# Loads that wait for the fourth tile ahead, the last x before a decode's end, and a ring of banks moved by one

## The chip, the cores and the metric

The kernel runs on one core of a Trainium2 chip. The metric is the device time of one execution in microseconds (us); three runs of the kernel before gave a median of 846.01 us (845.52 to 846.19).

## What is computed

```python
def reference(q, k, v, w_in, w_out, w_in2, w_out2):     # q, k, v: (4, 8, 576, 64)
    gamma = 1 - 2.0 ** (-5 - arange(8))                 # one per head
    D = where(i >= j, gamma[:, None, None] ** (i - j), 0)
    x = ((q @ k.T) / 8 * D) @ v                         # retention: attention with a decay, no softmax
    x = x.transpose(0, 2, 1, 3).reshape(2304, 512)
    x = relu(x @ w_in) ** 2 @ w_out                     # 512 -> 2048 -> 512
    h = x @ w_in2
    return (h * clip(h + 3, 0, 6) / 6) @ w_out2
```

The weights come as 64-bit floats and are turned into 32-bit ones on the chip.

## The kernel before

**Three parts.** First the retention, in ten units: two pairs of batches, and for each pair five stretches of the sequence (four of 128 positions, one of 64). Then the first MoE block, in four passes (`FIRST`) over 16 chunks of the hidden dimension. Then the second block, in three passes (`SECOND`) with seven products for eight. The order of every engine's instructions is the order in which the program writes them (a manual schedule); waits between engines are put in where a tile is written or read.

**A unit of the retention.** `load_qk` and `load_kv` bring a tile of keys and queries for the scores (128 x 1024 floats, 512 KB) and a tile of keys and values, one of each for both batches of the pair. `scale_keys` multiplies the keys of a kv tile in place by the decay, on POOL (line 283). `scores` makes the products of keys and queries (PE, line 322) and DVE multiplies them with the decay (line 326). `values` multiplies these with the values (line 338), adds the product of scaled keys and values to the running sums (line 346, which reads what POOL scaled), and from the second stretch on adds the earlier stretches' part (line 354). `to_x` lets DVE write the result to `xall` (line 372). The main loop runs `scores(u)` ahead of `values(u - 1)`; after it come `values` and `to_x` of unit 9, the last parts of the decode of the second tile of `w_in` (`parts1`, on DVE lines 183 and 189), and the first products of the MoE (`emit_h`, line 439).

**Loads.** All of them are issued by SP in the order of the list `order`: the qk and kv tiles, two tiles of `w_in` among them, and five weight tiles at the end. `load_on(done)` issues the loads whose place has been given back by unit `done`; the first call issues all that need nobody's place. The semaphores of DMAs go round eight, so each DMA waits until the one eight before it has landed. A tile of `w_in` takes four DMAs, the last kv tile of a pair two.

**Banks.** Scores and values take PSUM banks in turn (`next_bank`) from a ring of seven (0 to 6); bank 7 holds the running sums. After the retention the ring is banks 4 to 7. The first pass of the MoE writes its products to banks 6 and 7 and sums its results in banks 0 to 5 (the last two, `ytail`, for the 256 positions beyond 512). In the second pass the first two chunks take banks 6 and 7, and from the third on they take banks from the ring. The ring's counter runs on over both parts.

```python
ring["n"] = 7                        # before the first unit
...
p = values(UNITS - 1)                # after the loop over the units
parts1.pop(0)()
to_x(UNITS - 1, p)
load_on(UNITS)
...
ring.update({"from": 4, "n": 4})
```

Of the kernel before, what the change touches and what calls it, by code (L numbers as in the profile page):

```python
# [9 lines left out]
F32 = mybir.dt.float32  # L10
# [65 lines left out]
def retention_moe_moe2(ctx, tc, qk, qk_last, kv, w_in, w_out, w_in2, w_out2, consts, out):  # L76

    nc = tc.nc
# [10 lines left out]
    const = pool("const", 1)  # L89
# [29 lines left out]
    def bank(i, shape, name):  # L119
        return banks.tile(shape, F32, tag=f"b{i}", name=name)  # L120

    ring = {"at": 0, "from": 0, "n": 6}

    def next_bank(shape, name):
        ring["at"] += 1
        return bank(ring["from"] + ring["at"] % ring["n"], shape, name)


    staged = {}
# [74 lines left out]
    UNITS = (B // 2) * NTB  # L204
# [5 lines left out]
    def unit(u):  # L210

        p, i = divmod(u, NTB)
        return 2 * p, i, min(C, S - C * i)

    def make_decays():

        for e, engine in enumerate((nc.vector, nc.gpsimd)):
            engine.tensor_tensor(
                out=decay[:, e], in0=mask.unsqueeze(1).to_broadcast([128, HP, C]),
                in1=gv[:, e].unsqueeze(2).to_broadcast([128, HP, C]), op=ALU.mult,  # L220
            )
# [9 lines left out]
    def half(i):  # L231
        return slice(64 * i, 64 * i + 64)
# [3 lines left out]
    def space(u, k, which):  # L236

        b, i, n = unit(u)
        s = u // NTB * (2 * TILES + 1) + 2 * i + k
        if AHEAD <= s < AHEAD + WIDE:  # L240
            if not wide:
                wide.append(place("xr", [128, 2 * WIDE, 1024], F32, "early"))
            return wide[0][:, 2 * (s - AHEAD) + which]
        tags = TOKENS[s if s < AHEAD else (s - WIDE) % len(TOKENS)]
        name = ("qkt", "kvt")[which]
        if tags is None:
            return wop.tile([128, 1024], F32, tag="wo", name=name)
        return place(tags[which], [128, 1024], F32, name)

    def load_qk(u, k):  # L250
        b, i, n = unit(u)
        t = space(u, k, 0)
        if n == C:
            nc.sync.dma_start(out=t, in_=qk[b + k, i])
            data[u]["qk", k] = t.rearrange("p (e a t) -> p e a t", e=2, a=HP)
            return
        t = t.rearrange("p (b f) -> p b f", b=2)
        nc.sync.dma_start(out=t, in_=qk_last[b:b + 2].rearrange("b p e a t -> p b (e a t)"))
        for e in range(2):
            data[u]["qk", e] = t[:, e].rearrange("p (e a t) -> p e a t", e=2, a=HP)  # L260

    def load_kv(u, k):
        b, i, n = unit(u)
        t = space(u, k, 1)
        if n == C:
            t = t.rearrange("p (e h d) -> p e h d", e=2, h=H)
            nc.sync.dma_start(out=t, in_=kv[b + k, C * i:C * i + n])
            data[u]["k", k], data[u]["v", k] = t[:, 0], t[:, 1]
            return
        for e in range(2):  # L270
            nc.sync.dma_start(
                out=t[half(e), :H * D], in_=kv[b + e, C * i:, 1].rearrange("t h d -> t (h d)")
            )
        data[u]["v", 0] = t[:, :H * D].rearrange("p (h d) -> p h d", h=H)

    def scale_keys(u):
        b, i, n = unit(u)
        if n < C:
            return
        gk = cst[:, C_GK + H * i:][:, :H]  # L280
        for k in range(2):
            keyt = data[u]["k", k]
            nc.gpsimd.tensor_tensor(
                out=keyt, in0=keyt, in1=gk.unsqueeze(2).to_broadcast([128, H, D]), op=ALU.mult
            )
# [3 lines left out]
    def column(a, e):  # L289

        return a % 2 if a < 2 else 1 - (a % 2 ^ e)
# [36 lines left out]
    def values(u):  # L328
        b, i, n = unit(u)
        r = rets.pop(u)  # L330
        p = [next_bank([128, 2, 2 * n], "vps").rearrange("p c (k t) -> p c k t", k=2) for j in range(2)]
        if i == 0:
            sums_of[b] = bank(7, [128, 2, HP, D], "sps")
        for k in range(len(r)):
            for a in PAIRS:
                for e in range(2):
                    to = p[a // 2][half(e ^ a // 2), column(a, e)]
                    nc.tensor.matmul(
                        out=to[:, k] if n == C else to.rearrange("p k t -> p (k t)"),
                        lhsT=data[u]["v", k][:, 2 * a + e, :], rhs=r[k][e][:, a],  # L340
                        start=k == 0 and a % 2 == 0, stop=i == 0, skip_group_check=True,
                    )
            if n == C:
                for a in range(HP):
                    for e in range(2):
                        nc.tensor.matmul(
                            out=sums_of[b][half(e), k, a, :],
                            lhsT=data[u]["k", k][:, 2 * a + e, :], rhs=data[u]["v", k][:, 2 * a + e, :],
                            start=i == 0 and k == 0 and a == 0, stop=True, skip_group_check=True,
                        )  # L350
        for k in range(2) if i else ():
            for a in PAIRS:
                for e in range(2):
                    nc.tensor.matmul(
                        out=p[a // 2][half(e ^ a // 2), column(a, e), k],
                        lhsT=every[half(e), i % 2, k, a, :], rhs=data[u]["qk", k][half(e), 1, a],
                        start=False, stop=True, skip_group_check=True,
                    )
        if n == C:
            for a in range(HP):  # L360
                nc.scalar.activation(
                    out=every[:, (i + 1) % 2, :, a], in_=sums_of[b][:, :, a], func=ACTF.Copy,
                    scale=cst[:, C_GS + HP * i + a:][:, :1],
                )
        return p

    def to_x(u, p):
        b, i, n = unit(u)
        for j in range(2):
            own = slice(2 * j, 2 * j + 2)  # L370
            x = xall[:, own].rearrange("p k (b s) -> p b k s", b=B)[:, b:b + 2, :, C * i:C * i + n]
            nc.vector.tensor_tensor(  # L372
                out=x, in0=p[j].rearrange("p c k t -> p k c t"), in1=gq[:, own, :n].unsqueeze(1).to_broadcast([128, 2, 2, n]), op=ALU.mult
            )
# [268 lines left out]
    def pair(j, p, flip, between):  # L643
# [83 lines left out]
    coming = halves + [  # L727
        (0, 1, 2 * p + e, w) for p in range(NPAIR) for e, w in ((0, 0), (1, 0), (0, 1), (1, 1))
    ]
# [7 lines left out]
    with tc.manual_schedule():  # L737
# [6 lines left out]
        order = [("qk", 0), ("kv", 0), ("qk", 1)]  # L744
        for u in range(2, UNITS):
            order += [("qk", u), ("kv", u - 1)]
        order = [(kind, u, k) for kind, u in order + [("kv", UNITS - 1)] for k in range(2 if unit(u)[2] == C else 1)]
# [4 lines left out]
        def release(kind, u, k):  # L752

            s = u // NTB * (2 * TILES + 1) + 2 * unit(u)[1] + k
            if kind == "w" or s < AHEAD + WIDE + 2:
                return -1
            return FREED[s]
# [4 lines left out]
                   == (s - len(TOKENS) if s - len(TOKENS) >= AHEAD + WIDE else s - len(TOKENS) - WIDE))  # L762
            for s in range(AHEAD + WIDE + 2, (B // 2) * (2 * TILES + 1))
        }
        loads_w = [2]

        def load_on(done):

            while order:
                kind, u, k = order[0]  # L770
                if release(kind, u, k) > done or kind == "w" and len(order) <= 5 and done < UNITS - 3:
                    return
                order.pop(0)
                if kind == "w":
                    load()
                else:
                    (load_qk if kind == "qk" else load_kv)(u, k)

        load_qk(0, 0)
        load_qk(0, 1)  # L780
        del order[:2]
        nc.scalar.dma_start(out=cst[:, :C_GQ], in_=consts[:, :C_GQ])
        rows = place("t6", [128, C_END - C_GQ], F32, "rows")
        nc.scalar.dma_start(out=rows[:2], in_=consts[:2, C_GQ:])
        load_on(-1)

        warm = bank(6, [128, 256], "warm")
        for _ in range(WARM):
            nc.tensor.matmul(out=warm, lhsT=zeros[:, :128], rhs=zeros, start=True, stop=True)

        ring["n"] = 7
        make_decays()
        scale_keys(0)
        lows, parts0, parts1 = [], [], []
# [32 lines left out]
        for u in range(UNITS):  # L827
# [6 lines left out]
            if u != 1:  # L834
                v = max(u - 1, 0)
                p = values(v)
# [5 lines left out]
                make_last_decay()  # L842
            at(u, True)
        p = values(UNITS - 1)
        parts1.pop(0)()
        to_x(UNITS - 1, p)
        load_on(UNITS)
        next_load()
        split_in(0, 1, nc.gpsimd)
# [81 lines left out]
        for k in range(total):  # L931
            j, p = divmod(k, NPAIR)
# [80 lines left out]
```

## Time and profile before

| | |
|---|---|
| median of three runs | 846.01 us |
| the profiled execution, its own time | 846.26 us |
| its span, from the first to the last instruction | 844.5 us |
| busy in the span: PE, DVE, ACT, POOL | 98%, 62%, 54%, 17% |
| mean granted clock of TensorE | 0.999 |
| moved by DMA | 183.47 MB, mean 217 GB/s |

The span leaves out 1.8 us of the execution around it. PE is TensorE's matmuls, PEld its weight loads, DVE VectorE, ACT ScalarE, POOL GpSimd, SP the engine that issues the loads. In a timeline a row gives the start, the time to the end, the engine, the line, the operation, what it writes and reads, the number of instructions merged, and in brackets the engine's idle time before it with what ended it; "issue" is time in which the engine waited for nothing that the profile shows.

### The profile page before, as it was taken

To read this page: it belongs to the slowest core of one execution; us is meant where nothing else is said; L and a number is where in the kernel's file an instruction comes from. 1 tells how busy PE (TensorE), PEld (TensorE's weight loads), DVE (VectorE), ACT (ScalarE), POOL (GpSimd) and SP (SyncE) were. 2 spreads that over 40 slices of the span, in tenths; PEclk is the share of its full clock that TensorE was granted. 3 is DMA by queue.
4 is the path that set the end of the run, shared out by engine and by line. 5 is a ranking of instruction groups with operands and counts; after the bars stand their busy time and mean duration, and the time that the engine had idled before them with its cause. 6 is when DMAs were issued, how large, how long until landed. Compare 5 with 4: busy or idle time off the path is not lost.

```text
span 844.5 us, 13270 instructions
## 1 busy us (share of the span) xinstructions
PE 830.8 (98%) x4932; PEld 721.9 (85%) x4932; DVE 521.9 (62%) x875; ACT 454.4 (54%) x847; POOL 142.5 (17%) x122
## 2 busy tenths in 40 slices
PE   9889999999999999999999999999999999999997
PEld 7888888888888888888888889898898889889886
DVE  5778777775777777687665644545644546534433
ACT  1238767676677777777665433345433345433332
POOL 2352323231432233233320000000000000000000
PEclk9999999999999999999999999999999999999999
DMA  9991666565678777877686464562864552954622
GB/s 362 370 324 58 194 181 194 181 189 192 244 263 308 254 246 264 301 277 253 231 289 239 173 220 164 175 211 88 310 226 163 189 197 88 331 206 160 205 95 76
DMA packets 67413, 183.47 MB, mean 217 GB/s; under 512 B 6802, under 2 KB 23314, under 8 KB 67348
## 3 DMA queue, kind: packets, MB, share of 16 engines
q1 hardware_dynamic: 66768, 181.69, 62.3%
q10 hardware_dynamic: 580, 0.92, 0.3%
q8 instruction: 39, 0.64, 0.3%
q14 instruction: 26, 0.21, 0.1%
HBM read 146.41 MB, written 36.18 MB: 216 GB/s over the span
## 4 chain that ended last, share of the span: by engine, by line
PE 88%; DMA 8%; ACT 2%; DVE 1%; issue 0%; POOL 0%; SPq 0%; ACTq 0%; DVEq 0%
PE yps L623 23%; PE hps L439 22%; PE yps L482 21%; PE hps L657 20%; DMA qkt<-in_qk_dram 3%; PE ytail L482 3%; DMA stage<-in_w_in_dram 2%; DMA qkt<-in_qk_last_dram 1%; DMA cst<-in_consts_dram 1%; DMA wo<-kept 0%; ACT r L460 0%; ACT r L459 0%; DVE w L189 0%; ACT a L170 0%; ACT r L171 0%
## 5 line engine op out<-in xcount | busy, mean ns | idle before, releaser
L623 PE MATMUL yps<-wo,g 128*128 128x512 f32 x864 | 226.4, 394 | 0.2 <-DMA wo<-kept 0.2
L482 PE MATMUL yps<-g,wo 128*128 128x512 f32 x768 | 195.5, 392 | 0.4 <-POOL wo L196 0.4
L623 PEld LDWEIGHTS yps<-wo,g 128*128 128x128 f32 x864 | 159.5, 188 | 24.2 <-ACT v L668 0.4
L482 PEld LDWEIGHTS yps<-g,wo 128*128 128x128 f32 x768 | 140.0, 188 | 28.0 <-POOL wo L196 3.6
L439 PE MATMUL hps<-xring,win 128*128 128x512 f32 (+1 forms) x720 | 153.4, 361 | 1.8 <-DVE xall L372 1.5
L439 PEld LDWEIGHTS hps<-xring,win 128*128 128x128 f32 x720 | 123.1, 189 | 23.1 <-DVE xall L372 1.6
L657 PE MATMUL hps<-xlast,win 128*128 128x384 f32 x576 | 116.1, 336 | 0.0
L657 PEld LDWEIGHTS hps<-xlast,win 128*128 128x128 f32 x576 | 103.2, 188 | 8.8
L676 DVE TENSOR_TENSOR u<-hps,u 128x384 f32<-128x384 f32 x48 | 26.8, 558 | 107.3 <-PE hps L657 107.3
L465 DVE TENSOR_TENSOR g<-r,g 128x512 fp32r<-128x512 f32 x64 | 47.2, 737 | 70.0 <-ACT g L461 69.6
L657 PE MATMUL hps<-xop,win 128*128 128x384 f32 x432 | 87.2, 336 | 0.0
L459 ACT ACTIVATE r<-hps 128x512 f32<-128x512 f32 x80 | 43.9, 549 | 73.8 <-PE hps L439 73.8
L670 ACT ACTIVATE g<-c 128x384 fp32r<-128x384 f32 x72 | 37.8, 525 | 84.3 <-DVE c L669 84.3
L657 PEld LDWEIGHTS hps<-xop,win 128*128 128x128 f32 x432 | 77.5, 188 | 6.6
L668 ACT ACTIVATE v<-c,three 128x384 f32<-128x384 f32 x72 | 44.4, 617 | 32.7 <-DVE c L676 31.4
L439 PE MATMUL hps<-xown,win 128*128 128x512 f32 x240 | 59.8, 390 | 0.7 <-ACT xall L491 0.7
L195 ACT ACTIVATE win<-w 128x512 fp32r<-128x512 f32 x64 | 39.7, 620 | 26.7 <-DVE w L189 26.7
L174 DVE TENSOR_SCALAR a<-a 128x512 f32<-128x512 f32 x64 | 38.8, 606 | 24.0 <-ACT a L170 24.0
L439 PEld LDWEIGHTS hps<-xown,win 128*128 128x128 f32 x240 | 44.8, 188 | 10.1 <-ACT xall L491 0.9
L695 ACT ACTIVATE c<-hps 128x384 f32<-128x384 f32 x24 | 11.8, 492 | 76.7 <-PE hps L657 76.7
L460 ACT ACTIVATE r<-r 128x512 f32<-128x512 f32 x80 | 47.2, 590 | 2.5
L669 DVE SCALAR_TENSOR_TENSOR c<-v,c 128x384 f32<-128x384 f32 x72 | 40.0, 555 | 13.4 <-ACT v L668 13.4
(94 smaller groups left out, 980.9 us busy)
## 6 DMA issues: line engine op xcount, KB each, us to landing
wo<-kept SPq DMA_DIRECT2D x96, 512.0 KB, 5.0
win<-kept SPq DMA_DIRECT2D x72, 512.0 KB, 3.7
kept<-ready SPq DMA_DIRECT2D x40, 512.0 KB, 4.2
stage<-in_w_out_dram SPq DMA_DIRECT2D x32, 512.0 KB, 4.2
kept<-wo SPq DMA_DIRECT2D x16, 512.0 KB, 5.1
stage<-in_w_in_dram SPq DMA_DIRECT2D x16, 512.0 KB, 4.1
qkt<-in_qk_dram SPq DMA_DIRECT2D x13, 512.0 KB, 7.9
kvt<-in_kv_dram SPq DMA_DIRECT2D x13, 512.0 KB, 8.5
```

The costliest lines, as they stand in the source:

```text
L174: nc.vector.tensor_scalar(out=a, in0=a, scalar1=LEAST, scalar2=MOST, op0=ALU.max, op1=ALU.min)
L195: lambda: nc.scalar.activation(out=hi, in_=src, func=ACTF.Copy),
L439: nc.tensor.matmul(out=h, lhsT=w[:, wp, kk * 128:kk * 128 + 128], rhs=xs[pos, kk][xp][:, o:o + n], start=m == 0, stop=m == 3 * KD - 1,)
L459: nc.scalar.activation(out=r, in_=hs[k], func=ACTF.Relu)
L460: nc.scalar.activation(out=r, in_=r, func=ACTF.Square)
L465: nc.vector.tensor_tensor(out=lo, in0=src, in1=hi.bitcast(F32), op=ALU.subtract)
L482: nc.tensor.matmul(out=p, lhsT=w[:, wp, m * 128:m * 128 + 128], rhs=g[pos, c][k][:, gpart, :size], start=c == 0 and e == 0 and not (k and ...
L623: nc.tensor.matmul(out=p, lhsT=gt[m // 3][:, gpart, m % 3 * 128:][:, :128], rhs=w[:, wp], start=first and e == 0, stop=last and e == 2,)
L657: nc.tensor.matmul(out=to, lhsT=wl[k][:, half, wp, o], rhs=x[:, xp, f], start=first and m == 0, stop=last and m == 5, skip_group_check=True,)
L668: nc.scalar.activation(out=v, in_=c, func=ACTF.Relu, bias=three)
L669: nc.vector.scalar_tensor_tensor(out=c, in0=v, scalar=6.0, in1=c, op0=ALU.min, op1=ALU.mult)
L670: nc.scalar.activation(out=hi, in_=c, func=ACTF.Copy)
```

## The change

Three edits. **Markers:** from the seventh tile on, each load of the list is preceded by a copy of one element (4 bytes) from the tile loaded four before it into a small tile `seen`, on the same queue. The copy reads that tile, so SP waits until it has landed. There are 37 of them. **Order:** `to_x` of the last unit stands ahead of the last part of the decode. **Ring:** its counter starts at 1 instead of 0.

```diff
     def load_qk(u, k):
...
-            return
+            return t
...
-        loads_w = [2]
+        landing = []
+        seen = const.tile([1, 64], F32, name="seen")
+
+        def behind():
+
+            n = len(landing)
+            if n >= 6:
+                nc.sync.dma_start(out=seen[:, n:][:, :1], in_=landing[n - 4])
...
                 order.pop(0)
+                behind()
                 if kind == "w":
+                    name = coming[0][1:]
                     load()
+                    t = staged[name].bitcast(F32)
                 else:
-                    (load_qk if kind == "qk" else load_kv)(u, k)
+                    t = (load_qk if kind == "qk" else load_kv)(u, k)
+                landing.append(t[:1, :1])
...
-        load_qk(0, 0)
-        load_qk(0, 1)
-        del order[:2]
+        for k in range(2):
+            kind, u, k = order.pop(0)
+            landing.append(load_qk(u, k)[:1, :1])
...
-        ring["n"] = 7
+        ring.update({"at": 1, "n": 7})
...
         p = values(UNITS - 1)
+        to_x(UNITS - 1, p)
         parts1.pop(0)()
-        to_x(UNITS - 1, p)
         load_on(UNITS)
```

In the listings below the number behind a tile's name tells tiles of one name apart, and DMAHW0 to DMAHW7 are the eight DMA semaphores.

First SP, from the seventh load on (the first six are the same). Before:

```order
L254 DMA qkt_107<-in_qk_dram 128x1024 [waits DMAHW0_49]
L254 DMA early_109<-in_qk_dram 128x1024 [waits DMAHW1_49]
L267 DMA kvt_111<-in_kv_dram 128x1024 [waits DMAHW2_49]
L267 DMA kvt_113<-in_kv_dram 128x1024 [waits DMAHW3_49]
L254 DMA early_109<-in_qk_dram 128x1024 [waits DMAHW4_49]
```

Now:

```order
L776 DMA seen_92<-kvt_100 1x1 [waits DMAHW4_49,DMAHW0_49]
L254 DMA qkt_109<-in_qk_dram 128x1024 [waits DMAHW1_49]
L776 DMA seen_92<-kvt_102 1x1 [waits DMAHW5_49,DMAHW2_49]
L254 DMA early_112<-in_qk_dram 128x1024 [waits DMAHW3_49]
L776 DMA seen_92<-qkt_104 1x1 [waits DMAHW6_49]
L270 DMA kvt_115<-in_kv_dram 128x1024
L776 DMA seen_92<-qkt_106 1x1 [waits DMAHW7_49]
L270 DMA kvt_118<-in_kv_dram 128x1024
```

Between two loads stands a marker, which waits for the tile four loads back (kvt_100 is the third tile loaded, qkt_109 the seventh).

Second POOL, the scaling of the keys of units 0 and 1. Before:

```order
L283 TENSOR_TENSOR kvt_99<-kvt_99,cst_81 128x512 [waits DMAHW4_49]
L283 TENSOR_TENSOR kvt_101<-kvt_101,cst_81 128x512 [waits DMAHW5_49]
L283 TENSOR_TENSOR kvt_111<-kvt_111,cst_81 128x512 [waits DMAHW2_49]
L283 TENSOR_TENSOR kvt_113<-kvt_113,cst_81 128x512 [waits DMAHW3_49]
```

Now:

```order
L287 TENSOR_TENSOR kvt_100<-kvt_100,cst_81 128x512 [waits DMAHW4_49,DMAHW0_49]
L287 TENSOR_TENSOR kvt_102<-kvt_102,cst_81 128x512 [waits DMAHW5_49,DMAHW2_49]
L287 TENSOR_TENSOR kvt_115<-kvt_115,cst_81 128x512 [waits DMAHW5_49,DMAHW4_49]
L287 TENSOR_TENSOR kvt_118<-kvt_118,cst_81 128x512 [waits DMAHW7_49,DMAHW6_49]
```

The second semaphore is that of the marker that reads the same tile: the scaling writes the element that the marker reads, and the marker is written ahead of it in the program. So it is for the twelve full kv tiles of units 0 to 3, 5 and 7. For units 6 and 8 the scaling is written first, and the marker, and with it the load behind it, waits for POOL.

Third, where the retention ends, DVE. Before:

```order
L372 TENSOR_TENSOR xall_83<-vps_919,cst_81 128x2x2x128 [waits PE_49]
L183 SCALAR_TENSOR_TENSOR a_882<-stage_675,a_882 128x512 [waits DMAHW2_49,DMAHW1_49,DMAHW7_49,DMAHW0_49,DVE_49]
L189 ISA w32_530<-a_882,r_883 128x1024 [waits DVE_49,Activation_49]
L372 TENSOR_TENSOR xall_83<-vps_975,cst_81 128x2x2x64 [waits PE_49]
L372 TENSOR_TENSOR xall_83<-vps_976,cst_81 128x2x2x64 [waits PE_49]
L174 TENSOR_SCALAR a_1008<-a_1008 128x512 [waits Activation_49]
```

Now:

```order
L376 TENSOR_TENSOR xall_83<-vps_957,cst_81 128x2x2x128 [waits PE_49]
L183 SCALAR_TENSOR_TENSOR a_920<-stage_704,a_920 128x512 [waits DMAHW5_49,DMAHW4_49,DMAHW6_49,DMAHW3_49,DVE_49]
L376 TENSOR_TENSOR xall_83<-vps_1013,cst_81 128x2x2x64 [waits PE_49]
L376 TENSOR_TENSOR xall_83<-vps_1014,cst_81 128x2x2x64 [waits PE_49]
L189 ISA w32_554<-a_920,r_921 128x1024 [waits DVE_49,Activation_49]
L174 TENSOR_SCALAR a_1046<-a_1046 128x512 [waits Activation_49]
```

The decode's end (line 189) stands behind the two writes of the last x. On PE, the third chunk of the second pass (products `hps` from `xown`) began with a wait for ACT before; with the ring moved it takes another bank, and its first wait is one for DVE at its third matmul, as it had before too.

## Rows read from the trace of the kernel before

**Rows 1.** The page, busy time of each engine.

```profile
PE 830.8 (98%) x4932; PEld 721.9 (85%) x4932; DVE 521.9 (62%) x875; ACT 454.4 (54%) x847; POOL 142.5 (17%) x122
```

**Rows 2.** Stretches: length, busy time (instructions) of each engine, granted clock, DMA share, GB/s.

```profile
5.00:64.00 59.00, 52.55 (x1123) 47.97 (x1122) 41.42 (x72) 15.58 (x43) 25.78 (x24) 1.00 1.01 361
64.00:87.00 23.00, 21.96 (x122) 18.79 (x122) 18.94 (x31) 20.08 (x39) 6.92 (x5) 1.00 0.29 88
...
210.00:844.00 634.00, 630.04 (x2989) 547.33 (x2987) 371.97 (x632) 328.95 (x597) 75.02 (x64) 1.00 0.61 215
```

**Rows 3.** The page, DMA queues: packets, MB, share of 16 engines.

```profile
q8 instruction: 39, 0.64, 0.3%
```

**Rows 4.** Timeline of PE, the five stalls put down to "issue".

```profile
30.37 0.88 PE L338 MATMUL vps<-ret,early 128*64 128x128 f32 x12 [1.68 <-issue]
...
37.01 0.46 PE L354 MATMUL vps<-qkt,state 64*64 64x64 f32 x15 [0.83 <-issue]
...
43.71 0.51 PE L322 MATMUL aps<-qkt 64*128 64x128 f32 x3 [0.34 <-issue]
...
50.60 0.60 PE L322 MATMUL aps<-qkt 64*128 64x128 f32 x6 [0.77 <-issue]
...
56.77 0.45 PE L305 MATMUL aps<-qkt 64*64 64x64 f32 x14 [0.71 <-issue]
```

**Rows 5.** DMA queues in 27.8 to 29.2, 34.5 to 36, and 58.5 to 60 us.

```profile
q8 instruction: 1, 0.02, 4.8%
...
q8 instruction: 1, 0.02, 4.6%
...
q8 instruction: 1, 0.02, 3.9%
```

**Rows 6.** Timeline, units 0 and 1: POOL's scaling, PE's reading, SP's issues.

```profile
7.55 1.04 POOL L283 TENSOR_TENSOR kvt<-kvt,cst 128x512 f32<-128x512 f32 x1 [0.88 <-DMA kvt<-in_kv_dram]
...
9.86 0.63 PE L346 MATMUL sps<-kvt 128*64 128x64 f32 x16
...
11.34 0.33 SPq L267 DMA_DIRECT2D early<-in_kv_dram  x1
...
16.51 1.04 POOL L283 TENSOR_TENSOR kvt<-kvt,cst 128x512 f32<-128x512 f32 x1 [6.64 <-DMA kvt<-in_kv_dram]
...
16.58 1.09 PE L338 MATMUL vps<-ret,kvt 128*64 128x128 f32 x16 [0.97 <-DMA kvt<-in_kv_dram]
```

**Rows 7.** Timeline, units 7 and 8: POOL, and PE's reading of the last scaled keys.

```profile
50.13 1.81 POOL L196 TENSOR_TENSOR xring<-xall,xring 128x768 fp32r<-128x768 f32 x1
...
55.75 1.04 POOL L283 TENSOR_TENSOR kvt<-kvt,cst 128x512 f32<-128x512 f32 x1 [0.53 <-DMA kvt<-in_kv_dram]
...
59.53 0.63 PE L346 MATMUL sps<-kvt 128*64 128x64 f32 x16
```

**Rows 8.** Timeline, the end of the retention and the first product of the MoE.

```profile
62.16 0.69 PE L354 MATMUL vps<-qkt,state 64*64 64x64 f32 x32
62.44 0.68 DVE L183 SCALAR_TENSOR_TENSOR a<-stage,a 128x512 int32<-128x512 int32 x1
63.26 0.69 DVE L189 CUSTOM_DVE_ANT_0 w<-a,r 128x1024 uint16<-128x1024 uint16 x1
63.87 0.75 DVE L372 TENSOR_TENSOR xall<-vps,cst 128x256 f32<-128x256 f32 x2
63.99 0.63 ACT L195 ACTIVATE win<-w 128x512 fp32r<-128x512 f32 x1 [2.57 <-DVE w L189]
64.34 4.11 PE L439 MATMUL hps<-xring,win 128*128 128x512 f32 x21 [1.49 <-DVE xall L372]
...
67.41 0.60 ACT L459 ACTIVATE r<-hps 128x512 f32<-128x512 f32 x1 [0.54 <-PE hps L439]
```

**Rows 9.** Timeline, the third chunk of the second pass.

```profile
206.39 0.60 ACT L491 ACTIVATE xall<-ytail 128x512 f32<-128x512 f32 x1 [0.28 <-PE ytail L482]
...
207.04 0.50 PE L439 MATMUL hps<-xown,win 128*128 128x512 f32 x1 [0.69 <-ACT xall L491]
```

More of the change, by code (lines that the diff above doesn't have):

```diff
@@ L255, in load_qk @@
             data[u]["qk", k] = t.rearrange("p (e a t) -> p e a t", e=2, a=HP)
-            return
+            return t
+        whole = t
         t = t.rearrange("p (b f) -> p b f", b=2)
@@ L260, in load_qk @@
             data[u]["qk", e] = t[:, e].rearrange("p (e a t) -> p e a t", e=2, a=HP)
+        return whole
     def load_kv(u, k):
@@ L265, in load_kv @@
         if n == C:
+            whole = t
             t = t.rearrange("p (e h d) -> p e h d", e=2, h=H)
@@ L268, in load_kv @@
             data[u]["k", k], data[u]["v", k] = t[:, 0], t[:, 1]
-            return
+            return whole
         for e in range(2):
@@ L274, in load_kv @@
         data[u]["v", 0] = t[:, :H * D].rearrange("p (h d) -> p h d", h=H)
+        return t
     def scale_keys(u):
```

## The prediction

> **What bounds the kernel now.** I read the page's busy times first: TensorE is busy 830.8 of 844.5 us [rows 1], so only some 14 us of the span can be won without taking matmul work away. The stretches then say where they lie [rows 2]. From 210 us on PE is busy 630.04 of 634 us. In 5 to 64 us, the attention part, it is busy 52.55 of 59, and the DMA engines are full (share 1.01, 361 GB/s). In 64 to 87 us ACT is busy 20.08 of 23. The granted clock is 1.00 in all three, the higher of the two levels (2.4 GHz), so no term here is a clock term. Nothing of the change touches the work after 87 us except one bank.
>
> In the attention part the idle time of PE has two kinds. One is a wait for a load: 0.97 us at 16.58 [rows 6]. The other is put down to "issue", a wait for nothing that the profile shows: 1.68, 0.83, 0.34, 0.77 and 0.71 us, ending at 30.37, 37.01, 43.71, 50.60 and 56.77 [rows 4], 4.3 us in all. They come 6 to 7 us apart, in the middle of runs of matmuls whose operands are there. The queue table names the likely cause: 39 transfers of instructions, 0.64 MB [rows 3], 16 KB each; PE's 9,864 matmuls and weight loads [rows 1] make about 253 for each. One such transfer lies in 27.8 to 29.2 us and one in 34.5 to 36 us [rows 5], each ending 1 to 2 us before a stall ends [rows 4]. So PE runs out of instructions, and the next 16 KB don't begin to move until about 4.2 us after the last stall's end (30.37 to the window from 34.5). Where the loads thin out, the transfer lies in 58.5 to 60 us [rows 5], about 2 us after the stall that ended at 56.77, and no stall follows. The fetch shares the DMA engines with up to eight queued loads, and fewer queued loads should let it start sooner.
>
> **The change, part by part.**
>
> *The markers, what they give.* A load now follows a 4-byte copy that waits for the tile four loads back, so about four loads of 512 KB stand in the queues instead of eight. A load lands every 1.28 us (7.55 to 11.34 is three of them [rows 6]), so the four hold 5.1 us of work. A new load reaches the engines after two issues of about 0.33 us and its own start, while three loads, 3.8 us, still stand queued: the engines should stay fed, and I cost lost bandwidth at nothing; its cover is these 3.8 us. If the fetch then waits 2 instead of 4 us, all five stalls go: **-4.3 us**. Its bounds are -4.3 and 0.
>
> *The markers, what they cost.* There are 37, each a small issue on SP, which waits between loads anyway: nothing. But a marker reads the first element of a tile that POOL later scales in place. By the second listing of the change above, the scaling of the keys of units 0 to 3, 5 and 7 now waits for the marker as well as for the load. The marker is issued when the tile has landed and stands behind the three loads issued since, so it lands some 3.8 us later. Unit 0: POOL scaled at 7.55, when the tile landed; the third load behind that tile is the one whose landing released SP at 11.34. So the scaling runs from about 11.4 to 12.45, and the product that reads it, at 9.86 before [rows 6], starts **2.6 us** late. That makes the 0.97 us wait of unit 1 vanish (-1.0): its tile has long landed. Unit 1's scaling, 16.51 before, may come up to 3.8 us later and end at 21.35; PE, 1.6 us late, would want it at 19.2. If the copy stands on a DMA engine that is ahead, the wait is less; between 0 and 2.1 I take **1.0**. Units 2 and 3 then lie behind a PE that is 2.6 us late, and wait for nothing. By unit 5 the lost stalls have brought PE back, and units 5 and 7 may wait 0 to 1.5 us each; I take **0.5** twice. After unit 7 POOL still has its 1.81 us split [rows 7] ahead of the next keys. Sum of the attention part: -4.3 + 2.6 - 1.0 + 1.0 + 1.0 = **-0.7 us**. Its last product, 62.16 + 0.69 = 62.85 before [rows 8], ends near 62.15.
>
> The Trainium skill (DMA: Bandwidth & Descriptors, "Queues, rings and completion order") says that each DMA engine consumes its descriptors in ring order: by that the marker stands behind the loads, as I have it. No row of before shows a copy of this size.
>
> *The last x and the bank.* The first matmul of the MoE waited 1.49 us for DVE's write of the last x, since it reused that bank [rows 8]. With the ring moved by one its bank was read units ago, and it starts when PE is free. But ACT sets the pace there. Its weight copy at 63.99 waits for the decode that ended at 63.26 + 0.69 = 63.95, and then four decode copies run to 66.87. The decode step now stands behind the last x (0.75 us), which can start only at 62.4, when DVE's step before it is done: 62.4 + 0.75 + 0.69 gives about 63.9, no earlier than before. So ACT is free at 66.87 as before, and only the 0.54 us that it then waited for PE [rows 8] go. **The 0.7 us shrink to 0.55**; PE's 1.49 us turn into waits for ACT, whose bank read gates the next groups.
>
> *The bank in the second block.* At 207.04 PE had waited 0.69 us for ACT's copy out of a tail bank (at 206.39) [rows 9]. With the ring one further this group takes a bank last read two groups earlier, and the first matmul's wait for ACT is gone from PE's order: **-0.7 us**, and PE is the bound from there [rows 2].
>
> Sum: -0.55 - 0.7 = -1.25 us. The profiled execution took 846.26 us (844.5 and 1.8 around it), 0.25 above the median of 846.01. From the median: **844.7 us**.
>
> **The rivals.** A: *the marker lands at once*, because its engine is ahead or it overtakes. Then the key waits are 0 and the loads bound the part: unit 8's second keys, scaled from 55.75 to 56.79, were read at 59.53 [rows 7], so 2.7 us can be won there. With the 0.15 us lost at ACT and 0.7 us of the bank: **842.7**. For it: the DMA engines needn't be equally late; against: all are full.
>
> B, the slower side: *the fetch starts no sooner*. If an engine alternates between the fetch's queue and the loads' queue, its wait depends on what one turn holds and not on how many loads stand behind. Then the 4.3 us of stalls stay and the key waits come on top: 844.7 + 4.3 = **849.0**. It decides if the fetch still starts about 4 us after a stall's end. For it: with eight loads, 10 us of work, the fetch waited about 4.2, so it does overtake some; against: where fewer and smaller loads were queued it waited about 2 [rows 4, 5]. The Trainium skill (same page and section) has this as its rule: an engine round-robins between queues and switches only at packet boundaries, of some 9 to 17 descriptors. By that rule queue depth would not matter and the time would be B's; that the wait exceeded a load's 1.28 us neither fits one short packet nor excludes longer ones.
>
> C: *the markers change nothing that ends last*; gains and waits cancel and only the bank of the second block counts: 846.0 - 0.7 = **845.3**.
>
> The Trainium skill (Runtime: NRT & Kernel Launch, "Instruction fetch mechanics") calls fetches of 16 KiB blocks mostly hidden; the trace agrees on the size and, with five stalls in this part, disagrees on the hiding.
>
> **How the numbers follow.** Forecast 0.42, with 843.7 to 846.3 as its own range (each of the two unsure key terms at its ends); A 0.20; B 0.26; C 0.12. A measurement of this kernel tells about 0.2% (1.7 us) from no change, so faster means below 844.3. That is A and somewhat under half of the forecast's range: 0.38. Slower is B: 0.26. The rest, 0.36, is within. The range reaches just past A to 842.0 and up to B's 849.0.
>
> **What would show it.** Right: no "issue" idle time above 0.3 us on PE between 5 and 64 us; POOL's first scaling starts near 11.4 instead of 7.55; the last product of the attention ends near 62; the first MoE matmul follows it without a gap; PE's 0.69 us gap near 206 is gone. POOL's first scaling near 9 would speak for A; stalls of 0.7 us and more, a block of instructions apart, and a last product after 65, for B. Wrong altogether: a DMA share well under 0.95 in the attention part, which would mean that four loads don't keep the engines fed.

## The result and the profile after

The changed kernel took 854.06 us in the median of five runs (853.05 to 854.76), the kernel before, run beside it, 845.52 (845.15 to 846.19). The ratio is 1.0092, with a 95% interval of 1.0080 to 1.0103: slower by 8.5 us, where I had forecast a gain of 1.3 and no case above 849. The profiled execution of the changed kernel has a span of 852.1 us, 7.6 more than before. Two executions far off the rest, 2129.73 us of run 4 below and 1024.75 of the kernel before, are left out of every figure.

The page, busy time of each engine; PE has 1.6 us more work than in [rows 1], which is the same work at a lower clock in places:

```profile
PE 832.4 (98%) x4932; PEld 723.0 (85%) x4932; DVE 523.2 (61%) x875; ACT 454.4 (53%) x847; POOL 143.4 (17%) x122
```

The stretches of the changed kernel (length, busy time and instructions of PE, PEld, DVE, ACT and POOL, granted clock, DMA share, GB/s):

```profile
5.00:64.00 59.00, 47.41 (x926) 42.70 (x930) 35.48 (x59) 11.02 (x31) 19.70 (x18) 0.94 0.93 317
...
9.00:12.20 3.20, 0.43 (x8) 0.19 (x4) 0.00 (x0) 0.04 (x1) 1.04 (x1) 0.85 1.02 396
12.20:16.00 3.80, 3.77 (x50) 3.65 (x50) 1.25 (x2) 0.04 (x1) 1.04 (x1) 0.50 0.93 370
20.00:35.00 15.00, 13.47 (x318) 12.38 (x314) 10.17 (x19) 2.28 (x8) 5.55 (x6) 1.00 0.92 303
...
64.00:87.00 23.00, 20.48 (x281) 17.89 (x272) 19.78 (x32) 17.73 (x37) 10.96 (x10) 1.00 0.46 136
210.00:844.00 634.00, 633.85 (x3012) 551.12 (x3011) 374.47 (x636) 332.68 (x604) 75.28 (x64) 1.00 0.61 214
```

Against [rows 2] the loss lies in the attention part. In 5 to 64 us PE is busy 47.41 us instead of 52.55 and gets through 926 matmuls instead of 1123. The DMA engines, full before, moved 317 GB/s instead of 361, their share fell from 1.01 to 0.93, and the granted clock from 1.00 to 0.94. What PE waited for there, in the view of waits (what waited, for what: us in total, times, longest):

```profile
PE sps L350 <- POOL kvt L287: 9.4, 4, 3.3
PE sps L350 <- POOL early L287: 1.9, 1, 1.9
PE vps L342 <- POOL ret L304: 0.2, 1, 0.2
```

No "issue" row is left: the five stalls of [rows 4] are gone. All that PE waits for is keys that POOL has still to scale, 11.3 us, and POOL waited for the markers. (The view names a load for one of POOL's waits, the one before the scaling at 45.39; but SP issued that tile's marker at 40.62, after the tile had landed, so there too it is the marker that came late.) Its timeline (start, us, engine, line, operation, idle time before with what ended it):

```profile
11.13 1.04 POOL L287 TENSOR_TENSOR kvt<-kvt,cst 128x512 f32<-128x512 f32 x1 [4.48 <-DMA seen<-kvt]
...
19.55 1.04 POOL L287 TENSOR_TENSOR kvt<-kvt,cst 128x512 f32<-128x512 f32 x1 [6.11 <-DMA seen<-kvt]
```

These answer to 7.55 and 16.51 of [rows 6]. What followed on PE in unit 0, from its timeline:

```profile
8.34 1.09 PE L342 MATMUL vps<-ret,kvt 128*64 128x128 f32 x16
12.23 1.12 PE L350 MATMUL sps<-kvt 128*64 128x64 f32 x16 [2.80 <-POOL kvt L287]
13.14 1.92 PE L342 MATMUL vps<-ret,kvt 128*64 128x128 f32 x16
14.85 1.07 PE L350 MATMUL sps<-kvt 128*64 128x64 f32 x16
15.85 3.98 PE L326 MATMUL aps<-qkt 64*128 64x128 f32 x48
```

The wait itself is 2.80 us, but behind it the same matmuls take longer: 1.12 us where the product of [rows 6] took 0.63, and so on for four groups. The stretch 12.2 to 16 above has a clock of 0.50, the lower level of 1.2 GHz, after a stretch in which PE was busy for 0.43 of 3.20 us. Over the four groups this adds 2.8 us (for each, its time less that of the same group before: 0.49, 0.88, 0.44 and 1.03).

The end of the retention, which answers to [rows 8]:

```profile
70.31 0.69 PE L358 MATMUL vps<-qkt,state 64*64 64x64 f32 x32
70.94 4.44 PE L443 MATMUL hps<-xring,win 128*128 128x512 f32 x24
71.66 0.74 DVE L376 TENSOR_TENSOR xall<-vps,cst 128x256 f32<-128x256 f32 x2
72.33 0.67 DVE L189 CUSTOM_DVE_ANT_0 w<-a,r 128x1024 uint16<-128x1024 uint16 x1
```

The last product starts at 70.31, 8.15 us later than before. The terms: stalls -4.33, unit 1's wait for its load -0.97, first matmuls 0.6 shorter, key waits +11.4, POOL's `ret` +0.2, lower clock +2.8; together +8.5, which leaves 0.4 to rounding and overlap. The first MoE matmul then follows without the gap of 1.49 us.

### The profile page after: what moved, and what is told of

Read it like the earlier page. It is cut to its first block, busy times and chain, and to the rows that moved or that the text cites. A ratio compares the mean times of both kernels' runs of the same rounds, so it can differ in the third digit from the quotient of the medians.

```text
span 852.1 us, 13333 instructions
## 1 busy us (share of the span) xinstructions
PE 832.4 (98%) x4932; PEld 723.0 (85%) x4932; DVE 523.2 (61%) x875; ACT 454.4 (53%) x847; POOL 143.4 (17%) x122
## 4 chain that ended last, share of the span: by engine, by line
PE 88%; DMA 6%; ACT 1%; POOL 1%; DVE 1%; SPq 1%; issue 1%; ACTq 0%; DVEq 0%; POOLq 0%
PE yps L627 24%; PE hps L443 21%; PE hps L661 21%; PE yps L486 20%; DMA kvt<-in_kv_dram 3%; PE ytail L486 2%; DMA qkt<-in_qk_dram 2%; POOL kvt L287 1%; SPq L776 1%; DMA early<-in_kv_dram 1%; DMA seen<-kvt 1%; DMA stage<-in_w_out_dram 0%; ACT r L171 0%; DVE a L183 0%; ACT r L464 0%
## 5 line engine op out<-in xcount | busy, mean ns | idle before, releaser
L195 ACT ACTIVATE win<-w 128x512 fp32r<-128x512 f32 x64 | 39.7, 620 | 28.0 <-DVE w L189 27.8
```

The lines of the kernel that those rows point to most:

```text
L195: lambda: nc.scalar.activation(out=hi, in_=src, func=ACTF.Copy),
```

## Experiments

In the records theory W is that the read of the key holds back the scaling and so makes the loss; its rival D, that four queued loads don't keep the DMA engines fed. Later records call the sharper form of D theory Q.

**1. Markers that read a value.** The tile is the same, the element one that POOL does not write, so the scaling no longer waits for the marker.

```diff
-                landing.append(t[:1, :1])
+                landing.append(t[:1, 512:513] if kind == "kv" and unit(u)[2] == C else t[:1, :1])
```

> The markers of the full kv tiles read the first value instead of the first key, which POOL does not write; all else as in the change. Theory W (the copy that reads a key holds back POOL's scaling until it has landed): no wait of POOL for a marker in units 0 to 3, PE's waits for scaled keys fall from 11.3 us to under 3, no fall of the clock at 9 to 18 us, last product of the retention near 60 us instead of 71, time 841 to 844 us. Rival D (four loads ahead starve the queues, so the loads themselves come late): DMA share still near 0.93, last product after 66 us, time 849 us or more.

Measured: 852.4 us, ratio 1.0063 (1.0041 to 1.0084). The key waits are all but gone and the clock is 1.00 throughout, but most of the loss stays. The stretch of 5 to 64 us, then the three longest of PE's waits in the timeline:

```profile
5.00:64.00 59.00, 50.35 (x1011) 43.75 (x1010) 38.29 (x67) 14.38 (x38) 20.75 (x19) 1.00 0.90 317
```

```profile
15.10 1.16 PE L326 MATMUL aps<-early 64*128 64x128 f32 x16 [1.04 <-DMA early<-in_qk_dram]
23.77 1.09 PE L342 MATMUL vps<-ret,kvt 128*64 128x128 f32 x16 [1.32 <-DMA kvt<-in_kv_dram]
...
36.37 1.25 PE L326 MATMUL aps<-qkt 64*128 64x128 f32 x16 [1.85 <-DMA qkt<-in_qk_dram]
```

PE now waits for the loads themselves, at the same 317 GB/s. Theory W falls for the greater part. The read of the key may add to it, 854.06 us with it and 852.4 without, but the two intervals of the ratio overlap between 1.0080 and 1.0084, so the times alone don't show it.

**2. Order and ring alone.** The kernel before, with the last x moved and the ring started at 1, and no markers.

```diff
-        ring["n"] = 7
+        ring.update({"at": 1, "n": 7})
...
+        to_x(UNITS - 1, p)
         parts1.pop(0)()
-        to_x(UNITS - 1, p)
```

> The kernel before with the order of the last x and the ring moved by one, without markers. Theory W: the retention is as before, PE's 0.7 us gap at 206 us is gone, the swap at the end of the retention is worth between -0.5 and +0.5 us: 844.6 to 845.8 us. Rival O (these two edits carry the loss): 849 us or more.

Measured: 845.34 us, ratio 0.9992 (0.9982 to 1.0001): not told from no change, and no part of the loss.

**3. Markers alone**, with order and ring as before (the reverse of the diff above, on the changed kernel).

> The change with the order of the last x and the ring undone: markers alone. Theory W: the same waits for scaled keys as in the change, and the 0.7 us gap near 206 us back: 854 to 855.5 us. Rival O: under 850 us.

Measured: 854.69 us, ratio 1.0091 (1.0068 to 1.0114). The markers carry the whole loss.

**4. Only unit 0 freed.** The markers of unit 0's kv tiles read a value, all others as in the change.

```diff
-                landing.append(t[:1, :1])
+                landing.append(t[:1, 512:513] if kind == "kv" and u == 0 else t[:1, :1])
```

> The change, but the two markers of unit 0's kv tiles read a value instead of a key: of the waits for scaled keys only that of unit 0 (2.8 us) is taken away. If the fall of the clock in 12 to 18 us comes from PE's idle time in that wait, it goes too (2.8 us more), and the sum of 5.6 us is partly taken back by later waits: 849 to 852 us, granted clock 1.00 in 5 to 20 us. If the clock falls for another reason, it falls again and the time is 852 us or more.

Measured: 854.71 us, ratio 1.0096 (1.0075 to 1.0117): a miss, nothing was won. Unit 0 no longer waits and the clock stays at 1.00 from 5 to 20 us, but a longer wait stands in unit 1, again with a fall of the clock behind it (0.77 in 20 to 35 us). PE's timeline:

```profile
22.54 1.12 PE L350 MATMUL sps<-kvt 128*64 128x64 f32 x16 [4.01 <-POOL kvt L287]
```

One wait taken away alone was followed by another at a later tile, as one would expect where the loads set the pace.

**5. Markers that read a constant.** All 37 stay, but none waits for a tile.

```diff
-                nc.sync.dma_start(out=seen[:, n:][:, :1], in_=landing[n - 4])
+                nc.sync.dma_start(out=seen[:, n:][:, :1], in_=cst[:1, :1])
```

> All 37 markers stay, but each copies one constant that landed before the first load, so no marker waits for a tile. Theory Q (the loss is the short queue, and the markers shorten it by being transfers themselves: SP keeps at most eight unfinished transfers, and every second one is now a marker): the load still waits for the fourth load ahead of it; 849 to 855, 310 to 330 GB/s in 5 to 64 us, key waits gone, PE waiting for loads, at most 1 us of issue stalls. Rival R (the loss is what the markers read, the wait for the tile four loads back): without it eight loads stand queued again, 844 to 847, 350 GB/s and more, and the issue stalls of some 4 us are back. Rival S (the 37 issues of 0.585 us on SP are the loss): loads are then issued no faster than every 0.9 us, which is less than the 1.28 us of one load, so at most 1 us, 845 to 847.

Measured: 850.01 us, ratio 1.0049 (1.0037 to 1.0061). The stretch, PE's longest wait in the timeline, and the longest total among SP's waits:

```profile
5.00:64.00 59.00, 52.27 (x1031) 47.37 (x1032) 40.51 (x67) 14.40 (x38) 23.63 (x21) 0.94 0.94 326
```

```profile
34.58 1.25 PE L326 MATMUL aps<-qkt 64*128 64x128 f32 x16 [2.53 <-DMA qkt<-in_qk_dram]
```

```profile
SPq L270 <- DMA kvt<-in_kv_dram: 5.3, 8, 2.0
```

As theory Q had it: 326 GB/s, PE waits for loads, no stall. A marker is itself one of the eight DMAs that SP may have unfinished, so the 37 of them shorten the queue to four loads whatever they read; SP's loads wait here for earlier loads, though no marker reads a tile. Rival R falls (it had 844 to 847), and so does S (845 to 847), the theory that the loss is the issues. About 1 us of the loss goes with falls of the clock (0.66 in 35 to 40 us, 0.58 in 60 to 64): the executions with a mean clock of 1.000 and 0.999 took 849.06 and 849.66 us.

Two parts of the stretch differ; two lines from this run, two from the change and two from the kernel before:

```profile
10.00:20.00 10.00, 8.78 (x176) 8.15 (x176) 6.83 (x12) 1.48 (x6) 2.15 (x3) 1.00 1.03 399
25.00:35.00 10.00, 7.47 (x199) 6.79 (x196) 5.37 (x10) 3.40 (x10) 3.06 (x4) 1.00 0.90 277
...
10.00:20.00 10.00, 7.77 (x104) 7.65 (x106) 3.33 (x6) 1.14 (x4) 2.53 (x3) 0.66 0.96 361
25.00:35.00 10.00, 8.47 (x204) 7.74 (x202) 6.17 (x12) 1.14 (x4) 3.72 (x4) 1.00 0.88 273
...
10.00:20.00 10.00, 9.03 (x194) 8.56 (x194) 6.84 (x12) 1.46 (x6) 2.08 (x2) 1.00 1.03 408
25.00:35.00 10.00, 8.32 (x216) 7.58 (x212) 5.11 (x10) 3.42 (x10) 3.06 (x4) 1.00 1.05 335
```

In 10 to 20 us, where this run and the change load each tile in one DMA of 512 KB, four places for loads keep the engines full if nothing waits for a tile to land (399 GB/s, and 408 before); with the wait for the landing, as in the change, it is 361. In 25 to 35 us both fall short alike, 277 and 273 against 335. Just before, SP has issued a tile of `w_in` as four DMAs (256, 128, 64 and 64 KB), and it issues a kv tile as two of 128 KB. The ring counts DMAs, so its places then hold fewer bytes: an estimate from the trace of this run, bytes issued less bytes moved, gives about 1.2 MB queued in 10 to 20 us and 0.6 in 25 to 35. This reason fits both parts, but no run varies it alone.

**6 and 7. A marker before every second load**, reading a value, that waits for the fourth or for the sixth load back. Of eight unfinished DMAs some five are loads.

```diff
-            if n >= 6:
-                nc.sync.dma_start(out=seen[:, n:][:, :1], in_=landing[n - 4])
+            if n >= 6 and n % 2 == 0:
+                nc.sync.dma_start(out=seen[:, n:][:, :1], in_=landing[n - 6])
```

> A marker only before every second load, waiting for the fourth load back (a value, not a key), so four to five loads stand queued. Theory Q: between the change with values (852.4) and before: 847 to 851, 325 to 350 GB/s in 5 to 64 us, few issue stalls. Rival R: half of the waits are gone, 847 to 850. Rival S: 845 to 847. A run at 852 and more would say that one load more in the queue is worth nothing.

> A marker before every second load, waiting for the sixth load back; of eight unfinished transfers some five are loads. Theory Q: 845 to 849, 335 to 355 GB/s in 5 to 64 us; if the fetch of instructions gains from three loads fewer, issue stalls of 1 to 3 us in place of 4. Rival R: 844 to 846. If four loads were already as good as five, it would be 851 to 853.

Measured: 849.89 us, ratio 1.0049 (1.0033 to 1.0066), for the fourth load back; 845.32, ratio 0.9997 (0.9988 to 1.0005), for the sixth. The stretch of 5 to 64 us, first of the one, then of the other:

```profile
5.00:64.00 59.00, 52.30 (x1083) 46.35 (x1084) 41.93 (x69) 15.52 (x42) 23.86 (x24) 1.00 0.95 340
```

```profile
5.00:64.00 59.00, 54.94 (x1132) 49.35 (x1132) 44.03 (x73) 15.73 (x43) 25.45 (x24) 1.00 0.98 351
```

Both lie where theory Q put them; by the times rival R had them there too, and it is run 5 that speaks against R. The pair has the same markers on the same queue and differs in what they wait for: two loads less of waiting are worth 4.6 us. So with half of the markers the read counts as well. The issue on SP is no price of weight at this number, since the same 19 issues stand in both and the second loses nothing.

**8. A marker before every third load, sixth load back** (`n % 3 == 0` in the diff above, all else as there). Six of the eight are loads.

> A marker before every third load, waiting for the sixth load back; of eight unfinished transfers six are loads. Theory Q: 843.5 to 847, 345 to 360 GB/s in 5 to 64 us; issue stalls of 2 to 4 us remain, since most of the queue is back. This is the point at which a gain over the kernel before (845.5) could show, if fed engines and an early fetch go together at all; if they do not, it stands at 845 to 846 with the stalls of before.

Measured: 844.02 us, ratio 0.9978 (0.9969 to 0.9987): faster than both kernels. The stretch, and PE's stalls and the end of the retention in its timeline:

```profile
5.00:64.00 59.00, 55.16 (x1135) 49.72 (x1135) 43.81 (x73) 16.25 (x44) 25.27 (x24) 1.00 0.99 359
```

```profile
29.09 0.88 PE L342 MATMUL vps<-ret,early 128*64 128x128 f32 x12 [0.44 <-issue]
...
48.88 1.38 PE L326 MATMUL aps<-qkt 64*128 64x128 f32 x19 [1.10 <-issue]
...
60.62 0.69 PE L358 MATMUL vps<-qkt,state 64*64 64x64 f32 x32
61.25 4.47 PE L443 MATMUL hps<-xring,win 128*128 128x512 f32 x24
```

Fed engines, and two stalls of 1.54 us instead of five of 4.33 [rows 4]: the retention ends 1.54 us sooner than in [rows 8]. It ends hardly sooner than in run 2, though, which has no markers (60.62 against 60.69), and the intervals of the two ratios overlap between 0.9982 and 0.9987. That the thinned markers win anything beyond the moved order and ring is therefore not shown.

**9. The thinned markers alone**, without the moved x and ring.

> The thinned markers (before every third load, sixth load back, a value) without the moved x and the moved ring. Theory Q with the instruction stalls: the markers alone win by the shorter queue, 844 to 845.3 (the run with all parts, 844.0, plus the 0.7 us that order and ring gave by themselves), issue stalls of 1 to 2 us, 350 to 360 GB/s. Rival: the gain of the thinned markers hangs on the moved x and ring, since the work after the attention sets the pace: then 845.3 to 846.5, no different from before.

Measured: 845.17 us, ratio 0.9992 (0.9983 to 1.0001). By the time alone neither case is excluded. In the profiled execution the last product starts at 60.93, 1.2 us sooner than before, and then the gain is lost. PE's timeline and the stretch behind it:

```profile
63.52 10.22 PE L443 MATMUL hps<-xring,win 128*128 128x512 f32 x48 [1.90 <-DVE xall L376]
```

```profile
64.00:87.00 23.00, 22.71 (x122) 19.49 (x120) 17.47 (x29) 18.54 (x37) 5.84 (x5) 0.93 0.28 81
```

PE waits 1.90 us for the bank instead of 1.49, and behind the wait the clock falls (0.93 over the stretch, 0.62 in 63.5 to 67 us). In run 8, with the ring moved, the first product of the MoE follows at once. Not every execution loses the gain: of the twelve of run 9, six show a mean clock of 0.997 or 0.998 and took 845.41 to 846.58 us (the profiled one among them), and six show 1.000 and took 843.91 to 844.93; in run 8 all show 0.999 or 1.000. That the moved ring lets the sooner end through by sparing the wait and the fall of the clock is read from these; the intervals of the two ratios still overlap, between 0.9983 and 0.9987.

**10 and 11. Every fourth load, seventh back; every third load, fifth back** (otherwise as run 8).

> A marker before every fourth load, seventh load back, all else as the change; of eight unfinished transfers six to seven are loads. If six loads were the best depth, more of the issue stalls are back (2 to 4 us): 844.3 to 845.5, 355 to 361 GB/s. If the stalls stay as low as with six loads: 843 to 844.

> A marker before every third load, but it waits for the fifth load back; five to six loads queued. Theory Q: between the runs with markers at every second and every third load that wait for the sixth: 843.5 to 846, 345 to 358 GB/s, issue stalls of 0.5 to 1.5 us. At 848 and more, a wait for the fifth load back alone would starve the engines.

Measured: 844.76 us, ratio 0.9984 (0.9975 to 0.9993), stalls of 1.54 us; and 844.86, ratio 0.9989 (0.9980 to 0.9999), stalls of 0.83. In run 10 the stalls did not come back as its record had it; PE waited 1.7 us for one load instead. The intervals of 8, 10 and 11 overlap, so which of the three is best is not told.

**12. The kernel before, a second time.**

> The kernel before, unchanged, profiled a second time. My sum rests on the 4.3 us of issue stalls of one profiled execution; the kernel with only order and ring moved, whose instructions in the attention part are the same, showed 2.6 us. If the stalls belong to the kernel, they come again at 3.9 to 4.7 us, in five places. If they belong to the execution, they come out at 2 to 3.5 us, and the last product of the attention starts before 61.7 instead of 62.16, with the span shorter by as much.

Measured: 846.22 us in the one execution, span 844.4. Stalls of 1.51, 1.14, 0.34, 0.77 and 0.71 us, 4.47 in all, in the same five places; two rows of PE's timeline:

```profile
30.21 0.88 PE L338 MATMUL vps<-ret,early 128*64 128x128 f32 x12 [1.51 <-issue]
...
62.31 0.69 PE L354 MATMUL vps<-qkt,state 64*64 64x64 f32 x32
```

So the stalls came again at their full size, as the first bound had it. But run 2, with the same loads and matmuls in this part, shows 2.72 us of them. Whether the ring or the execution makes that difference stays open, and with it how much of the fewer stalls of runs 7 to 11 is due to the markers.

All runs in one table but 3 and 4, which mark every load as the change does. The number of loads is what the ring of eight leaves beside the markers, for tiles of one DMA; the last product is that of the retention, in the profiled execution.

| kernel | loads queued, waits for | GB/s, 5 to 64 us | stalls, us | last product | ratio |
|---|---|---|---|---|---|
| before | 8 | 361 | 4.33 | 62.16 | 1 |
| 2 | 8 | 360 | 2.72 | 60.69 | 0.9992 |
| 10 | 6.4, seventh | 360 | 1.54 | 61.37 | 0.9984 |
| 8 | 6, sixth | 359 | 1.54 | 60.62 | 0.9978 |
| 9 | 6, sixth | 358 | 1.33 | 60.93 | 0.9992 |
| 11 | 6, fifth | 358 | 0.83 | 60.47 | 0.9989 |
| 7 | 5.3, sixth | 351 | 1.26 | 61.20 | 0.9997 |
| 6 | 5.3, fourth | 340 | 2.04 | 64.61 | 1.0049 |
| 5 | 4, a constant | 326 | 0 | 66.53 | 1.0049 |
| 1 | 4, fourth, value | 317 | 0.15 | 68.84 | 1.0063 |
| the change | 4, fourth, key | 317 | 0 | 70.31 | 1.0092 |

## Why the prediction was wrong

**The step that failed** is "I cost lost bandwidth at nothing; its cover is these 3.8 us". With four loads queued the engines were not kept fed: 317 GB/s instead of 361. The premise under it, that the four hold 5.1 us of work, took every load for one DMA of 512 KB, landing every 1.28 us (the rows given for that, 7.55 and 11.34, make 1.26). Where that is so, in 10 to 20 us, the cover of three loads is too little beside the wait for a landing (361 GB/s, before 408; in run 5, without that wait, 399). Where some tiles come in two or four smaller DMAs, in 25 to 35 us, four places don't suffice even without it (273, run 5 277, before 335). Over the whole part, the table shows, six of the eight places must be left to loads to hold 358 GB/s and more. The sign that I had put down for "wrong altogether", a DMA share well under 0.95, is met in the second of these (0.88); the mean of the whole part is 0.93. Run 5 takes the read away and keeps the short queue, and 4 of the 8 us stay; run 8 gives most of the queue back and all of them go.

**"Units 2 and 3 ... wait for nothing", and 1.0 + 0.5 + 0.5 for the later units**, fell with it. Unit 0 was right: the scaling at 11.13 (I had 11.4), the wait 2.80 (2.6). Then unit 1 waited for nothing, but four more waits of 1.95, 3.34, 2.52 and 0.78 us stand at 35.50 (unit 3), 47.21 (unit 5), 60.72 and 63.06 (unit 7). The markers stand behind loads that are themselves late, so their lateness adds to that of the loads. Once the key reads are gone (run 1), the loads' own lateness shows in their place.

**"No term here is a clock term"** was wrong by 2.8 us: PE's idle time before 12.23 was followed by a stretch at the lower level.

**"All five stalls go: -4.3"** was right, and its reason is borne out: the fetch moves sooner. The block boundaries in the program stay the same (the stalls of run 8 stand at two of them), so the delay of the next fetch can be read: from the instruction behind the boundary (the fifth, eighteenth, sixteenth and fourteenth matmul of the groups below) to the half microsecond in which the next transfer moves. PE's timeline of the changed kernel, four groups that hold a boundary:

```profile
32.51 1.04 PE L342 MATMUL vps<-ret,early 128*64 128x128 f32 x16
...
40.16 0.69 PE L358 MATMUL vps<-qkt,state 64*64 64x64 f32 x32
...
49.27 2.06 PE L326 MATMUL aps<-qkt 64*128 64x128 f32 x32
...
55.12 2.06 PE L326 MATMUL aps<-qkt 64*128 64x128 f32 x32
```

The DMA queues of the changed kernel in 33.5 to 34, 43 to 43.5, 51 to 51.5 and 57 to 57.5 us (packets, MB, share):

```profile
q8 instruction: 1, 0.02, 15.4%
...
q8 instruction: 1, 0.02, 12.3%
...
q8 instruction: 1, 0.02, 11.1%
...
q8 instruction: 1, 0.02, 14.6%
```

With the boundaries worked out as 32.8, 40.5, 50.2 and 56.0, the delays are 0.7, 2.5, 0.8 and 1.0 us. Before, the fetches behind the first four stalls of [rows 4] moved in the half microseconds from 34.5, 41.0, 48.0 and 54.0: 4.1, 4.0, 4.3 and 3.4 us after the stall's end. All are good to half a microsecond. So rival B falls in this trace. The key waits help to hide a fetch as well, since they draw the boundaries apart (32.8 to 40.5 and 50.2 us, before 30.37 to 37.01 and 43.71); only the last, 5.8 us after the one before it, comes sooner than the 6 to 7 us of before. The rule behind it in the Trainium skill (DMA: Bandwidth & Descriptors, "Queues, rings and completion order"), that an engine goes round its queues packet by packet, doesn't by itself give a delay that depends on the loads queued; here it was 3.4 to 4.3 us with eight places for loads and 0.7 to 2.5 with four. With six it is no clear step between: in run 8 one fetch still moved 4.4 us late (boundary near 41.6, transfer in the half microsecond from 46), the one before the stall of 1.10 us, and the other three 0.9 to 2.6 us. The price was paid elsewhere: 11.4 us of key waits and 2.8 us of lower clock against 4.3 us of stalls.

**The marker's landing** was right: issued at 7.71, released POOL at 11.13, 3.4 us later and not at once, so rival A falls. Its issue was not 0.33 us but 0.585. The view of the tile `seen` (durations of the issues in ns, least, median, most):

```profile
L776 SPq DMA_DIRECT2D seen<-kvt x12: 585/586/722, 7.7 to 57.9; - x12
```

**The last x and the bank.** The gap of 1.49 us at the first MoE matmul and the wait of 0.69 us at the bank of the second block [rows 9] are gone, as said. The 0.55 us at the first were not won: in run 2 it is 25.62 us from the start of the last product (60.69) to the `yps` product that waits for `wo` (86.31), before 24.86 (62.16 to 87.02); POOL's copy into `wo` ends that stretch in both, with PE waiting 0.60 and 0.43 us for it. That ACT sets the pace there was right: in run 2 PE waits for it 0.91 and 1.27 us, at 66.69 and 72.40. Of the 1.25 us for both, run 2 shows about 0.7 (its ratio of 0.9992), and its interval doesn't exclude that nothing was won.

The change is slower, then, because it buys an early fetch of instructions with the queue that feeds the DMA engines, at four loads instead of eight. With six, and the moved order and ring, the kernel is 0.2% faster than before (run 8).

## What to carry to other kernels

A queue's depth is both a load's cover and another transfer's delay: count it in bytes, for a ring counts a small DMA like a large one, shorten it in steps and read GB/s beside the stalls, since below some depth the loss is steep (here 4.6 us between two kernels that differ only in how far back the wait reaches). A marker that is itself a transfer takes a place in the ring of semaphores, so it shortens the queue twice, and a marker that reads what an engine writes in place makes that engine wait too. A wait costs more than its length where PE's clock falls behind it.

## What the runs showed that I had not expected

The clock did not follow the length of the wait. In the changed kernel the wait of 2.80 us at 12.23 was followed by a clock of 0.50, that of 3.34 us at 47.21 by a clock of 1.00 (47 to 51 us). In run 3 a wait of 3.34 us at 45.06 was followed by 0.60 (45 to 49 us), and in run 9 one of 1.90 us by 0.62. What decides it, these rows don't tell.

A transfer of 4 bytes takes SP 0.585 us to issue, more than the 0.33 us of a 512 KB load in [rows 6].
